# Layer-norm means one step later, chunk 0's variance at step 6, DFT pieces two a step, four group sums scaled before they are added

## The chip, the core and the metric

The kernel runs on one core of one Trainium2 chip. The metric is the device time of one execution in microseconds (us). TensorE is called PE (its weight loads PEld), VectorE DVE, ScalarE ACT, GpSimd POOL and SyncE SP.

## The reference

Three blocks follow one another, with batch 4 and 544 tokens of 512 features (32 global and 512 local ones).

```python
x = attention(q_l, k_l, v_l, q_g, k_g, v_g)        # window of 32 and global tokens, 8 heads
h = np.maximum(x @ w_in, 0.0)                      # first feed-forward block, 512 -> 1024
gate = sigmoid(conv over tokens of h)
x = (h * gate) @ w_out
mixed = np.real(fft(fft(x, axis=1), axis=2))       # second block begins here
u = x + mixed
un = (u - mean(u)) / np.sqrt(var(u) + 1e-06)
ch = np.maximum(un @ w_ch1, 0.0) @ w_ch2           # 512 -> 2048 -> 512
return u + ch
```

## The kernel before

The matmuls run on pairs of numbers, a rounded high part and the rest as a low part, so each product is three matmuls (`mm3`). PE's and SP's instructions run in the order in which the program writes them; those of DVE, ACT and POOL are ordered by a scheduler, which simulates the program with priorities per kind of work. On the chip each engine then takes its own list strictly in that order.

**The Fourier transform.** `fft(b)` (L649) is a generator of 12 pieces for each of four batches. Its matmul pieces take PSUM banks `s` and `t` in turn (`fbank`, L646), and each bank has to be read by ACT and DVE (L674 and L675, L681 and L682, or L693 and L696, L703 and L706) before the next but one piece writes it. The last piece stores `ut` into `u_d[b]`. `fstep` (L859) runs one piece. The first pieces run beside the last steps of the first feed-forward block (the loop at L871), the rest in the last phase.

**The last phase** (the loop at L898) has 80 steps `v` and two more to drain. Tokens are cut into five chunks of 436 (the last 432), and step `v` takes one block of 128 hidden features `m` of a chunk `c`, from `plan`: chunk 0 with m 0 to 7 in steps 0 to 7, chunk 1 with 0 to 7 in steps 8 to 15, chunk 0 with 8 to 15, chunk 1 with 8 to 15, then chunks 2, 3 and 4 with 16 steps each. `c_g1(v)` (g1, L804) makes 12 matmuls into bank `pv` or `g1` (the trace calls the second `ps_g`), from which ACT (L817) and DVE (L818) make the two parts `hd`. `c_g2(v - 2)` (g2, L821) makes 12 matmuls from the `hd` of two steps before into the four banks a0 to a3 (`ps_a`). After m = 7 and m = 15 a group ends: for each of the four banks DVE multiplies by the chunk's `rs` into the one buffer `tmp` (L842) and adds that to the chunk's `uc` (L843), and after m = 15 SP stores `uc`. The next group's g2 can write a bank as soon as its multiplication is done.

**The layer norm.** `ln(c)` (L758) is a generator that advances once a step: it sums a chunk over its features into `cf` and `sr` (on POOL for chunks 1 to 4, on DVE for chunk 0), has PE form the mean over partitions with two matmuls by `ones` into bank `t` (L775), subtracts it (L778), squares, sums again, and has PE form the variance in bank `s` (L792), from which ACT's square root and DVE's reciprocal (L797) make `rs`. Chunk 0's runs beside the first feed-forward block and is finished at step 0:

```python
        while v == 0 and lnq:
            step(lnq)
```

Chunks 1 to 4 begin at steps 1, 26, 36 and 52. The tiles `uc` come from a pool of three, so chunk 2 is loaded (L755) into a tile that chunk 0's output leaves free.

**The remaining weights.** m = 8 to 15 of both weight matrices (`TAIL`, 16 tiles) need the memory that the transform uses. So at one step the loop empties the queue of pieces, closes the transform's pools and has SP load the 16 tiles (L181, `raw_v`, `raw_r`, `raw_o`); in the eight steps from there `make_c` unpacks two a step (ACT L166, L169, L202; POOL L167; DVE L173, L174, L203).

Of the kernel before, what the change touches and what calls it, by code (L numbers as in the profile page):

```python
# [34 lines left out]
TAIL = [x for m in range(8, 16) for x in (m, 16 + m)]  # L35
# [92 lines left out]
def fused_kernel(ctx: ExitStack, tc: tile.TileContext, d, out):  # L128
    nc = tc.nc
    pe, act, dve, gp, sp = nc.tensor, nc.scalar, nc.vector, nc.gpsimd, nc.sync  # L130

    def pri(c):
        k = PRIORITY.get(c, 0)
        return tc.high_priority(offset=k) if k else nullcontext()

    def prio(c):
        def deco(f):
            def g(*a, **k):
                with pri(c):
                    return f(*a, **k)  # L140
            return g
        return deco

    def mm(o, a, b, start, stop):
        return pe.matmul(o, a, b, start=start, stop=stop)  # L145

    def mm3(o, ah, al, bh, bl, start, stop):
        if al is None:
            mm(o, ah, bh, start, stop)
            return  # L150
        mm(o, al, bh, start, False)
        mm(o, ah, bl, False, False)
        mm(o, ah, bh, False, stop)
# [4 lines left out]
    def f32(ap):  # L158
        return ap.bitcast(F32)
# [31 lines left out]
    def unpack(pool, t, *how):  # L191
        if mags:
            mag = mags.pop(0)
            mags.append(mag)
        else:
            mag = pool.tile([128, 512], F32, tag="mag", name="mag", bufs=2)
        from_f64(t.rearrange("p (c b) -> p c b", b=2), mag, *how)
        return mag

    def put(pool, tag, val):  # L200
        t = pool.tile([128, 2, 512], F32R, tag=tag, name="w_" + tag)
        act.copy(t[:, 0], val)  # L202
        dve.tensor_sub(t[:, 1], val, f32(t[:, 0]))  # L203
        return t
# [12 lines left out]
    def bank(tag):  # L217
        return ps.tile([128, 512], F32, tag=tag, name="ps_" + tag)
# [247 lines left out]
    g_t, acc = {}, {}  # L466
# [255 lines left out]
    def c_slot(i):  # L722
        m = i % 16
        if m < 8:
            return (wp, f"w{m + (8 if i > 15 else 0)}")
        k = TAIL.index(i) - 13
        return (vp, f"v{i}") if k < 0 else (rb, ("r0", "r1", "o")[k])

    @prio("cv")
    def fetch_c(i):  # L730
        pool, tag = c_slot(i)
        if i not in kept:
            w_raw[i] = fetch(pool, tag, c_src(i))
            return
        t = pool.tile([128, 2, 512], F32R, tag=tag, name="w_" + tag)
        sp.dma_start(f32(t), kept[i])
        (ch2 if i > 15 else ch1)[i % 16] = t

    @prio("cv")
    def make_c(i):  # L740
        t = put(*c_slot(i), unpack(mp, w_raw.pop(i), gp, True))
        (ch2 if i > 15 else ch1)[i % 16] = t

    ln_t, uc_t, rs_t, cft = {}, {}, {}, []

    def width(c):
        return min(NT, B * S - NT * c)

    def load_uc(c):
        t = uc_t[c] = up.tile([128, 5, NT], F32, tag="u", name="uc")  # L750
        a, z = NT * c, NT * c + width(c)
        while a < z:
            b, o = divmod(a, S)
            n = min(z - a, S - o)
            sp.dma_start(t[:, 0:4, a - NT * c:a - NT * c + n], u_d[b][:, :, o:o + n])  # L755
            a += n

    def ln(c):  # L758
        n = width(c)
        ut = (uc_t[c] if c else u_t[0])[:, 0:4, 0:n]  # L760
        if c == 0:
            cft.append(up.tile([128, 5, NT], F32, tag="u", name="cf"))
        cf = cft[0][:, 0:4, 0:n]
        chl = xp.tile([128, 10, NT], F32R, tag="x", name="chl")
        ch, cl, sr = chl[:, 0:4, 0:n], chl[:, 4:8, 0:n], chl[:, 8:10, 0:n]
        eng = gp if c else dve
        eng.tensor_add(cf[:, 0:2], ut[:, 0:2], ut[:, 2:4])  # L767
        eng.tensor_add(cf[:, 0], cf[:, 0], cf[:, 1])
        act.copy(sr[:, 0], cf[:, 0])
        dve.tensor_sub(sr[:, 1], cf[:, 0], f32(sr[:, 0]))  # L770
        yield
        yield
        if c == 0:
            yield
        mu = bank("t")[:, 0:n]  # L775
        mm(mu, ones, sr[:, 1], True, False)
        mm(mu, ones, sr[:, 0], False, True)
        dve.tensor_sub(cf, ut, mu[:, None, :].to_broadcast([128, 4, n]))  # L778
        act.copy(ch, cf)
        eng.tensor_sub(cl, cf, f32(ch))  # L780
        ln_t[c] = (ch, cl)
        yield
        act.activation(cf, cf, AF.Square)
        yield
        eng.tensor_add(cf[:, 0:2], cf[:, 0:2], cf[:, 2:4])
        eng.tensor_add(cf[:, 0], cf[:, 0], cf[:, 1])
        yield
        act.copy(sr[:, 0], cf[:, 0])
        dve.tensor_sub(sr[:, 1], cf[:, 0], f32(sr[:, 0]))
        yield  # L790
        yield
        va = bank("s")[:, 0:n]  # L792
        mm(va, ones, sr[:, 1], True, False)
        mm(va, ones, sr[:, 0], False, True)
        rs = rs_t[c] = uc_t[c][:, 4, 0:n] if c else rs0
        act.activation(rs, va, AF.Sqrt, bias=eps)
        dve.reciprocal(rs, rs)  # L797
        yield
# [5 lines left out]
    def c_g1(v):  # L804
        if not 0 <= v < len(plan):
            return
        c, m = plan[v]
        ch, cl = ln_t[c]
        n = width(c)
        o = bank("g1" if m % 2 else "pv")[:, 0:n]  # L810
        w = ch1[m]
        for k in range(4):
            f = slice(128 * k, 128 * k + 128)
            mm3(o, w[:, 0, f], w[:, 1, f], ch[:, k], cl[:, k], k == 0, k == 3)
        hd = lw.tile([128, 2, NT], F32R, tag="hd", name="hd", bufs=3)[:, :, 0:n]
        with pri("cev"):
            act.activation(hd[:, 0], o, AF.Relu)  # L817
            dve.scalar_tensor_tensor(hd[:, 1], o, 0.0, f32(hd[:, 0]), op0=ALU.max, op1=ALU.subtract)  # L818
        hid[v] = hd

    def c_g2(v):  # L821
        if not 0 <= v < len(plan):
            return
        c, m = plan[v]
        n = width(c)
        first, last_ = (0, 8), (7, 15)
        if c > 1:
            first, last_ = (0,), (15,)
        if m in first:
            for e in range(4):  # L830
                acc[e] = bank(f"a{e}")[:, 0:n]
        hd = hid.pop(v)
        w = ch2[m]
        for e in range(4):
            f = slice(128 * e, 128 * e + 128)
            mm3(acc[e], w[:, 0, f], w[:, 1, f], hd[:, 0], hd[:, 1], m in first, m in last_)
        if m in last_:
            uc = uc_t[c]
            tmp = cft[0][:, 4, 0:n]
            for e in range(4):  # L840
                o = uc[:, e, 0:n]
                dve.tensor_mul(tmp, acc[e], rs_t[c])  # L842
                dve.tensor_add(o, o, tmp)  # L843
                if m == 15:
                    sp.dma_start(out[128 * e:128 * e + 128, NT * c:NT * c + n], o)

    fq = [fft(b) for b in range(4)]
    lnq = []

    def step(queue, name="ln"):  # L850
        while queue:
            try:
                with pri(name):
                    next(queue[0])
                return
            except StopIteration:
                queue.pop(0)

    def fstep(n=1):  # L859
        for _ in range(n):  # L860
            step(fq, "fft")
            for c, b in ((1, 1), (0, 2)):
                if b in u_d and c not in uc_t:
                    load_uc(c)
            if 0 in u_d and not lnq and not ln_t:
                lnq.append(ln(0))
                step(lnq)
# [28 lines left out]
    rs0 = lw.tile([128, NT], F32, name="rs0")  # L896
    vp = None
    for v in range(len(plan) + 2):  # L898
        if v < 8:
            for _ in range(3):  # L900
                fstep()
            if v < 4:
                make_c(20 + v)
        if v == 8:
            while fq:
                fstep()
            right.close()
            vp = ctx.enter_context(tc.tile_pool(name="vp", bufs=1, side="right"))
            for x in TAIL:
                fetch_c(x)  # L910
        if 8 <= v < 16:
            make_c(TAIL[2 * v - 16])
            make_c(TAIL[2 * v - 15])
        while v == 0 and lnq:
            step(lnq)
        if v in (1, 26, 36, 52):
            c = {1: 1, 26: 2, 36: 3, 52: 4}[v]
            if c > 1:
                load_uc(c)
            lnq.append(ln(c))  # L920
        step(lnq)
        c_g1(v)
        c_g2(v - 2)
# [42 lines left out]
```

## Time and profile before

| | |
|---|---|
| median of the three timed runs | 840.46 us (838.49 to 842.03) |
| the profiled execution: its own time | 836.21 us |
| its span in the profile | 834.4 us |
| PE busy | 778.8 us (93%) |
| PEld busy | 710.4 us (85%) |
| DVE busy | 477.1 us (57%) |
| ACT busy | 364.5 us (44%) |
| POOL busy | 173.7 us (21%) |

A share is an average over three blocks. The last phase begins at about 402 us and the transform's first pieces lie some 60 us before that. The granted clock is given as a share of TensorE's full 2.4 GHz, so 0.50 is its lower level of 1.2 GHz, and a value between is a stretch with both.

### The profile page before, as it was taken

The numbers are of one execution on the slowest core, as the hardware profiler recorded it, in microseconds if no ns is written. First come the engines' busy times: TensorE is split into PE (matmuls) and PEld (weight loads), VectorE is DVE, ScalarE is ACT, GpSimd is POOL, SyncE is SP. The second block draws the span as 40 slices with busy tenths as digits, with TensorE's granted clock in tenths as the row PEclk, the third lists the DMA queues.
The fourth block names the chain that finished last, engine by engine and source line by source line (L and its number), as shares of the span: only waits on it lengthen the run. The fifth ranks groups of instructions, "written<-read, shape, count | busy, mean of one in ns | idle before, by whom it ended". The sixth has DMA issues, their size and how long they took to land.

```text
span 834.4 us, 13622 instructions
## 1 busy us (share of the span) xinstructions
PE 778.8 (93%) x5272; PEld 710.4 (85%) x5272; DVE 477.1 (57%) x1162; ACT 364.5 (44%) x884; POOL 173.7 (21%) x219
## 2 busy tenths in 40 slices
PE   5769999999999999989799899997999999999996
PEld 3558888888889889979689798986999999999996
DVE  5899987768776786787854877132431232213112
ACT  6677776767676775543532852112112112111110
POOL 4555442222222230000222121004013003100000
PEclk9899999999999999999899999997999999999999
DMA  7842351254126441355323900020020011001001
GB/s 252 267 150 114 127 188 38 106 191 155 31 106 204 148 129 32 105 180 191 108 97 103 353 1 1 1 76 11 22 65 0 1 49 39 1 1 43 1 1 42
DMA packets 36896, 77.80 MB, mean 93 GB/s; under 512 B 3752, under 2 KB 22056, under 8 KB 36832
## 3 DMA queue, kind: packets, MB, share of 16 engines
q1 hardware_dynamic: 36000, 74.29, 26.2%
q0 software_dynamic: 832, 2.65, 1.4%
q8 instruction: 41, 0.67, 0.4%
q14 instruction: 23, 0.19, 0.1%
HBM read 62.11 MB, written 15.20 MB: 93 GB/s over the span
## 4 chain that ended last, share of the span: by engine, by line
PE 54%; DVE 19%; DMA 14%; ACT 8%; issue 2%; SPq 2%; POOL 0%; DVEq 0%; ACTq 0%; POOLq 0%
PE ps_a L145 24%; PE ps_g L145 13%; PE ps_pv L145 11%; DMA raw_r<-in_ch_dram 9%; PE ps_s L145 4%; PE ps_t L145 3%; ACT pb L320 2%; DVE pb L308 2%; DVE y L493 2%; DMA raw_w<-in_w_in_dram 2%; DVE y L494 2%; DVE mag L174 2%; DVE mag L173 1%; DMA raw_v<-in_ch_dram 1%; ACT mag L166 1%
## 5 line engine op out<-in xcount | busy, mean ns | idle before, releaser
L145 PE MATMUL ps_g<-x,w_w 128*128 128x256 f32 (+1 forms) x768 | 113.9, 298 | 1.3 <-ACT h L482 1.0
L331 POOL TENSOR_SCALAR pb<-pb,sm 128x224 f32<-128x224 f32 x128 | 84.5, 676 | 127.9 <-DVE sm L326 81.5
L145 PE MATMUL ps_a<-g,w_w 128*128 128x254 f32 (+1 forms) x768 | 110.9, 292 | 0.0
L145 PEld LDWEIGHTS ps_g<-x,w_w 128*128 128x128 f32 x768 | 100.9, 190 | 11.0 <-issue 7.7
L145 PE MATMUL ps_a<-hd,w_w 128*128 128x436 f32 (+1 forms) x480 | 102.7, 361 | 3.4 <-DVE cf L842 3.4
L145 PEld LDWEIGHTS ps_a<-g,w_w 128*128 128x128 f32 x768 | 101.1, 190 | 0.8 <-issue 0.7
L145 PEld LDWEIGHTS ps_a<-hd,w_w 128*128 128x128 f32 x480 | 89.7, 188 | 9.9 <-DVE cf L842 5.2
L818 DVE SCALAR_TENSOR_TENSOR hd<-ps_pv,hd 128x436 fp32r<-128x436 f32 (+1 forms) x40 | 24.4, 610 | 107.3 <-ACT hd L817 107.3
L818 DVE SCALAR_TENSOR_TENSOR hd<-ps_g,hd 128x436 fp32r<-128x436 f32 (+1 forms) x40 | 24.2, 606 | 95.3 <-ACT hd L817 95.3
L145 PE MATMUL ps_a<-hd,w_v 128*128 128x436 f32 (+1 forms) x360 | 77.4, 362 | 1.4 <-DVE cf L842 1.4
L817 ACT ACTIVATE hd<-ps_g 128x436 fp32r<-128x436 f32 (+1 forms) x40 | 21.3, 533 | 119.9 <-PE ps_g L145 119.8
L145 PEld LDWEIGHTS ps_a<-hd,w_v 128*128 128x128 f32 x360 | 67.8, 189 | 6.3 <-DVE cf L842 2.5
L817 ACT ACTIVATE hd<-ps_pv 128x436 fp32r<-128x436 f32 (+1 forms) x40 | 21.3, 533 | 117.5 <-PE ps_pv L145 117.4
L320 ACT ACTIVATE pb<-pb,sm 128x224 f32<-128x224 f32 x128 | 60.4, 474 | 11.9 <-DVE sm L308 11.8
L167 POOL TENSOR_SCALAR mag<-mag 128x512 f32<-128x512 f32 x48 | 35.3, 736 | 113.3 <-ACT mag L166 112.7
L145 PE MATMUL ps_pv<-chl,w_v 128*128 128x436 f32 (+1 forms) x240 | 52.9, 370 | 0.0
L767 POOL TENSOR_TENSOR cf<-uc 128x872 f32<-128x872 f32 (+1 forms) x4 | 8.3, 2068 | 212.5 <-DMA uc<-u_d 143.0
L145 PE MATMUL ps_g<-chl,w_w 128*128 128x436 f32 (+1 forms) x240 | 52.0, 367 | 0.0
L145 PE MATMUL ps_pv<-chl,w_w 128*128 128x436 f32 (+1 forms) x240 | 50.8, 360 | 0.0
L145 PE MATMUL ps_s<-qk 64*128 64x224 f32 (+1 forms) x144 | 37.1, 411 | 13.1 <-DMA qk<-in_qk_dram 4.1
L145 PEld LDWEIGHTS ps_pv<-chl,w_v 128*128 128x128 f32 x240 | 46.8, 195 | 2.8
L145 PEld LDWEIGHTS ps_g<-chl,w_w 128*128 128x128 f32 x240 | 46.2, 193 | 2.7
(220 smaller groups left out, 1462.5 us busy)
## 6 DMA issues: line engine op xcount, KB each, us to landing
v<-in_v_dram SPq DMA_DIRECT2D x16, 640.0 KB, 4.6
qk<-in_qk_dram SPq DMA_DIRECT2D x16, 464.0 KB, 6.1
raw_r<-in_ch_dram SPq DMA_DIRECT2D x14, 512.0 KB, 6.5
raw_v<-in_ch_dram SPq DMA_DIRECT2D x13, 512.0 KB, 9.3
kept<-w_o SPq DMA_DIRECT2D x12, 512.0 KB, 5.5
w_w<-kept SPq DMA_DIRECT2D x12, 512.0 KB, 3.2
qk<-in_qk_dram SPq DMA_DIRECT2D x16, 304.0 KB, 6.1
u_d<-u SPq DMA_DIRECT2D x4, 1088.0 KB, 5.3
```

The source lines that it names most:

```text
L145: return pe.matmul(o, a, b, start=start, stop=stop)
L166: act.activation(mag, f32(head), AF.Abs, scale=65536.0)
L167: (clamp or dve).tensor_scalar(mag, mag, TOP, 2.0, op0=ALU.min, op1=ALU.max)
L173: dve.scalar_tensor_tensor(val, val, 3, tail, op0=ALU.logical_shift_left, op1=ALU.bitwise_or)
L174: dve.scalar_tensor_tensor(val, head, -(2**31), val, op0=ALU.bitwise_and, op1=ALU.bitwise_or)
L308: anchor[i] = dve.tensor_tensor_reduce(out=pbs(i)[h][:, a, 0:224], in0=sb[h][:, a], in1=mask[:, 2 * where(i)[1] + a], scale=-0.125, scalar ...
L320: act.activation(p, p, AF.Exp, bias=sm[:, k:k + 1], scale=-1.0, accum_out=sm[:, 4 + k:5 + k])
L331: gp.tensor_scalar(p, p, sm[:, k:k + 1], 1.0, op0=ALU.mult, op1=ALU.mult)
L493: dve.scalar_tensor_tensor(y, hb[:, cc - 1:cc - 1 + n], convw2[:, m, 0:1], y, op0=ALU.mult, op1=ALU.add)
L494: dve.scalar_tensor_tensor(y, hb[:, cc + 1:cc + 1 + n], convw2[:, m, 2:3], y, op0=ALU.mult, op1=ALU.add)
L817: act.activation(hd[:, 0], o, AF.Relu)
L818: dve.scalar_tensor_tensor(hd[:, 1], o, 0.0, f32(hd[:, 0]), op0=ALU.max, op1=ALU.subtract)
```

## The change

1. All chunks now wait three steps between the sum and the mean, where chunks 1 to 4 waited two. Chunk 0's mean goes to bank `pv` and not `t`.
2. At a group end `tmp` becomes four buffers (the rows 0 to 3 of `cf`), and the program writes four multiplications and then four additions.
3. The transform's pieces come two a step in steps 0 to 8, where they came three a step in steps 0 to 7. The first four `make_c` stand at steps 2 to 5 and not 0 to 3, and the closing of the pools, the 16 loads and the unpacking all come one step later.
4. What is left of chunk 0's layer norm (its variance) runs at step 6 and not at step 0.

```diff
--- before.py
+++ after.py
@@ -770,9 +770,8 @@
         dve.tensor_sub(sr[:, 1], cf[:, 0], f32(sr[:, 0]))
         yield
         yield
-        if c == 0:
-            yield
-        mu = bank("t")[:, 0:n]
+        yield
+        mu = bank("t" if c else "pv")[:, 0:n]
         mm(mu, ones, sr[:, 1], True, False)
         mm(mu, ones, sr[:, 0], False, True)
         dve.tensor_sub(cf, ut, mu[:, None, :].to_broadcast([128, 4, n]))
@@ -836,11 +835,12 @@
             mm3(acc[e], w[:, 0, f], w[:, 1, f], hd[:, 0], hd[:, 1], m in first, m in last_)
         if m in last_:
             uc = uc_t[c]
-            tmp = cft[0][:, 4, 0:n]
+            tmp = cft[0][:, 0:4, 0:n]
+            for e in range(4):
+                dve.tensor_mul(tmp[:, e], acc[e], rs_t[c])
             for e in range(4):
                 o = uc[:, e, 0:n]
-                dve.tensor_mul(tmp, acc[e], rs_t[c])
-                dve.tensor_add(o, o, tmp)
+                dve.tensor_add(o, o, tmp[:, e])
                 if m == 15:
                     sp.dma_start(out[128 * e:128 * e + 128, NT * c:NT * c + n], o)
 
@@ -896,23 +896,25 @@
     rs0 = lw.tile([128, NT], F32, name="rs0")
     vp = None
     for v in range(len(plan) + 2):
-        if v < 8:
-            for _ in range(3):
-                fstep()
-            if v < 4:
-                make_c(20 + v)
-        if v == 8:
+        if v < 9:
+            fstep(2)
+            if 2 <= v < 6:
+                make_c(18 + v)
+        if v == 9:
             while fq:
                 fstep()
             right.close()
             vp = ctx.enter_context(tc.tile_pool(name="vp", bufs=1, side="right"))
             for x in TAIL:
                 fetch_c(x)
-        if 8 <= v < 16:
-            make_c(TAIL[2 * v - 16])
-            make_c(TAIL[2 * v - 15])
-        while v == 0 and lnq:
-            step(lnq)
+        if 9 <= v < 17:
+            make_c(TAIL[2 * v - 18])
+            make_c(TAIL[2 * v - 17])
+        if v == 0:
+            ln0, lnq = lnq, []
+        if v == 6:
+            while ln0:
+                step(ln0)
         if v in (1, 26, 36, 52):
             c = {1: 1, 26: 2, 36: 3, 52: 4}[v]
             if c > 1:
```

Three places show how this moves the engines' instructions. The first is PE's order at step 0. `c1` and `s1` are the transform's second tables, `ab` its intermediate, `ones` the mean's or variance's matrix, `chl` the normalized chunk and `w_w0`, `w_w1` its weights. Before:

```order
L145 MATMUL ps_s_5127<-c1_4344,ab_5026 128x274 x9
L145 MATMUL ps_t_5139<-s1_4345,ab_5026 128x274 x9
L145 MATMUL ps_s_5161<-chl_4664,ones_62 128x436 x2
L145 MATMUL ps_pv_5166<-chl_4664,w_w0_4471 128x436 x12
L145 MATMUL ps_s_5182<-c1_4344,ab_5026 128x274 x9
L145 MATMUL ps_t_5194<-s1_4345,ab_5026 128x274 x9
L145 MATMUL ps_s_5208<-c1_4344,ab_5026 1x274 x9
L145 MATMUL ps_g1_5237<-chl_4664,w_w1_4541 128x436 x12
```

and with the change:

```order
L145 MATMUL ps_s_5127<-c1_4344,ab_5026 128x274 x9
L145 MATMUL ps_pv_5139<-chl_4664,w_w0_4471 128x436 x12
L145 MATMUL ps_t_5155<-s1_4345,ab_5026 128x274 x9
L145 MATMUL ps_s_5169<-c1_4344,ab_5026 128x274 x9
L145 MATMUL ps_g1_5186<-chl_4664,w_w1_4541 128x436 x12
L145 MATMUL ps_t_5202<-s1_4345,ab_5026 128x274 x9
L145 MATMUL ps_s_5216<-c1_4344,ab_5026 1x274 x9
L145 MATMUL ps_pv_5240<-chl_4664,w_w2_4610 128x436 x12
```

The variance has left this place, and a g1 stands after the first, the third and the fifth of these pieces, where one stood after the second and one after the fifth.

The second is DVE's order at the end of chunk 0's second group (step 25). Before:

```order
L842 TENSOR_TENSOR cf_4663<-ps_a0_6076,rs0_5116 128x436
L818 SCALAR_TENSOR_TENSOR hd_6273<-ps_g1_6260,hd_6273 128x436
L843 TENSOR_TENSOR uc_5222<-uc_5222,cf_4663 128x436
L842 TENSOR_TENSOR cf_4663<-ps_a1_6077,rs0_5116 128x436
L843 TENSOR_TENSOR uc_5222<-uc_5222,cf_4663 128x436
L842 TENSOR_TENSOR cf_4663<-ps_a2_6078,rs0_5116 128x436
L843 TENSOR_TENSOR uc_5222<-uc_5222,cf_4663 128x436
L818 SCALAR_TENSOR_TENSOR hd_6321<-ps_pv_6308,hd_6321 128x436
L842 TENSOR_TENSOR cf_4663<-ps_a3_6079,rs0_5116 128x436
L843 TENSOR_TENSOR uc_5222<-uc_5222,cf_4663 128x436
```

and with the change:

```order
L840 TENSOR_TENSOR cf_4663<-ps_a0_6076,rs0_5116 128x436
L817 SCALAR_TENSOR_TENSOR hd_6273<-ps_g1_6260,hd_6273 128x436
L840 TENSOR_TENSOR cf_4663<-ps_a1_6077,rs0_5116 128x436
L843 TENSOR_TENSOR uc_5230<-uc_5230,cf_4663 128x436
L840 TENSOR_TENSOR cf_4663<-ps_a2_6078,rs0_5116 128x436
L840 TENSOR_TENSOR cf_4663<-ps_a3_6079,rs0_5116 128x436
L843 TENSOR_TENSOR uc_5230<-uc_5230,cf_4663 128x436 x3
L817 SCALAR_TENSOR_TENSOR hd_6321<-ps_pv_6308,hd_6321 128x436
```

Before, an addition follows each multiplication, and the last pair stands behind the next step's `hd_6321`; now all eight operations stand ahead of it, with one addition before the last two multiplications.

The third is PE's order at chunk 2's mean (`ones`). Before:

```order
L145 MATMUL ps_a_6327<-hd,w_v_5689 128x436 x3
L145 MATMUL ps_t<-chl,ones 128x436 x2
L145 MATMUL ps_pv<-chl,w_v_5825 128x436 x12
L145 MATMUL ps_a_6324<-hd,w_v_5741 128x436 x3
L145 MATMUL ps_a_6325<-hd,w_v_5741 128x436 x3
L145 MATMUL ps_a_6326<-hd,w_v_5741 128x436 x3
L145 MATMUL ps_a_6327<-hd,w_v_5741 128x436 x3
L145 MATMUL ps_g_6403<-chl,w_v_5869 128x436 x12
```

and with the change:

```order
L145 MATMUL ps_a_6327<-hd,w_v_5725 128x436 x3
L145 MATMUL ps_pv<-chl,w_v_5853 128x436 x12
L145 MATMUL ps_a_6324<-hd,w_v_5773 128x436 x3
L145 MATMUL ps_a_6325<-hd,w_v_5773 128x436 x3
L145 MATMUL ps_a_6326<-hd,w_v_5773 128x436 x3
L145 MATMUL ps_a_6327<-hd,w_v_5773 128x436 x3
L145 MATMUL ps_t<-chl,ones 128x436 x2
L145 MATMUL ps_g_6402<-chl,w_v_5897 128x436 x12
```

One whole step, a g1 and a g2, has moved ahead of the mean's two matmuls.

## Rows read from the trace of the kernel before

**Rows 1.** The page: the span.

```profile
span 834.4 us, 13622 instructions
```

**Rows 2.** Waits of PE from 340 us on: total us, times, longest.

```profile
PE ps_t L145 <- DVE chl L770: 7.7, 2, 6.7
PE ps_s L145 <- DVE u L696: 4.8, 1, 4.8
PE ps_a L145 <- DVE cf L842: 4.8, 5, 1.4
PE ps_t L145 <- DVE cf L778: 2.1, 1, 2.1
PE ps_t L145 <- DVE ab L675: 0.9, 1, 0.9
```

**Rows 3.** Chain of waits, one step: start us, us, what.

```profile
479.13 2.38 PE ps_g L145 x12
481.52 2.38 PE ps_a L145 x12
```

**Rows 4.** PE's timeline and windows (PE PEld DVE ACT POOL, clock) at chunk 0's mean.

```profile
365.83 0.66 PE L145 MATMUL ps_t<-chl,ones 128*128 128x436 f32 x2 [0.97 <-DVE chl L770]
368.56 0.36 PE L145 MATMUL ps_t<-c,fl 128*92 128x258 f32 x1 [2.06 <-DVE cf L778]
...
370.00:372.00 2.00, 2.00 (x11) 2.00 (x12) 1.78 (x1) 0.45 (x2) 0.00 (x0) 0.60 0.01 2
372.00:374.00 2.00, 2.00 (x11) 2.00 (x11) 0.61 (x3) 1.77 (x2) 0.00 (x0) 0.54 0.22 39
```

**Rows 5.** Windows of the stage with the DFT in steps 0 to 9.

```profile
414.00:416.00 2.00, 2.00 (x10) 1.35 (x8) 2.00 (x5) 0.12 (x1) 0.00 (x0) 0.50 0.00 0
416.00:418.00 2.00, 2.00 (x7) 1.82 (x6) 2.00 (x5) 1.10 (x2) 1.35 (x1) 0.50 0.00 0
...
401.00:471.00 70.00, 64.16 (x353) 58.34 (x352) 46.19 (x75) 30.45 (x53) 17.90 (x13) 0.95 0.40 139
```

**Rows 6.** Timelines of DVE (379 and 404 to 408 us) and of POOL (first, fourth).

```profile
379.59 0.72 DVE L658 TENSOR_TENSOR ff<-u 128x548 f32<-128x548 f32 x1
...
404.07 1.53 DVE L658 TENSOR_TENSOR ff<-u 128x548 f32<-128x548 f32 x1
408.17 2.86 DVE L797 RECIPROCAL rs<-rs 128x436 f32<-128x436 f32 x1
...
400.77 2.09 POOL L767 TENSOR_TENSOR cf<-uc 128x872 f32<-128x872 f32 x1 [69.48 <-DVE ff L655]
404.99 1.09 POOL L167 TENSOR_SCALAR mag<-mag 128x512 f32<-128x512 f32 x1
```

**Rows 7.** PE's last DFT piece; the chain's store; ACT's first raw weight.

```profile
445.65 0.55 PE L145 MATMUL ps_t<-c,ab 92*1 92x274 f32 x3
...
448.83 4.60 DMA u_d<-u
...
458.05 0.66 ACT L166 ACTIVATE mag<-raw_v 128x512 f32<-128x512 f32 x1 [3.38 <-DMA raw_v<-in_ch_dram]
```

**Rows 8.** DVE's timeline at chunk 0's last group end; windows after chunk 2's mean.

```profile
555.56 0.61 DVE L818 SCALAR_TENSOR_TENSOR hd<-ps_pv,hd 128x436 fp32r<-128x436 f32 x1 [0.38 <-ACT hd L817]
556.09 0.60 DVE L842 TENSOR_TENSOR cf<-ps_a,rs 128x436 f32<-128x436 f32 x1
556.73 0.61 DVE L843 TENSOR_TENSOR uc<-uc,cf 128x436 f32<-128x436 f32 x1
...
570.00:572.00 2.00, 2.00 (x7) 1.84 (x6) 1.76 (x1) 0.00 (x0) 0.00 (x0) 0.50 0.03 8
572.00:574.00 2.00, 2.00 (x8) 1.81 (x6) 0.21 (x1) 1.65 (x1) 0.00 (x0) 0.50 0.00 0
```

**Rows 9.** Chain of waits at the program's end, first and last of eight.

```profile
825.86 0.62 DVE cf L842
...
830.56 0.61 DVE uc L843
```

## The prediction

> **What bounds the kernel now.** I read the page first: a span of 834.4 us [rows 1], inside a profiled execution of 836.2 us; the three timed runs have a median of 840.5 us, 4.3 us more, so the sum below is made against 836.2 and then moved to the median. TensorE (PE) is busy nearly everywhere after 100 us, so what can be won late in the program is the time in which it stands still, and the time in which it is granted the lower clock. Second I read the list of PE's waits from 340 us to the end [rows 2]: five lines, 20.3 us in all, each of them ended by VectorE (DVE). Third, the chain of waits through an undisturbed step of the last phase [rows 3]: 12 matmuls of g1 in 2.38 us and 12 of g2 in 2.38 us, 4.76 us a step. The chain is PE with these holes in it. The reader should see that the holes belong to four places, which the four parts of the change touch one by one. Last I read PE's timeline and short windows around each hole for the granted clock.
>
> **Chunk 0's mean moves from bank t to bank pv.** Today PE computes it in bank t and the next DFT piece in t waits 2.06 us for the subtraction that reads the mean; a wait of 0.97 us stood just before [rows 4]. Behind both, the windows 370 to 372 and 372 to 374 have PE busy throughout at a granted clock of 0.60 and 0.54, largely the lower of its levels, 1.2 instead of 2.4 GHz: 2 x 0.40 + 2 x 0.46 = 1.7 us of work lost [rows 4]. In pv nothing of the DFT waits for that subtraction. The first wait (for the sum that feeds the mean) stays. Gain 2.1 + 1.7 = 3.8 at most, nothing at least; I take 3.0, near the upper end, because PE's waits list shows no other hole there, and keep 0.8 back because DVE has the same work in less time.
>
> **Chunk 0's variance to step 6 and DFT pieces two a step.** At steps 0 to 5 three pieces stand together, and PE's order begins with pieces s, t, the variance in s, one g1, then three pieces in a row. PE stops for 4.8 us until L696 has emptied bank s, and then works through 414 to 418 without a break at a granted clock of 0.50: 4 x 0.5 = 2.0 us lost [rows 2, 5]. Ahead of L696 in DVE's queue stood the reciprocal of chunk 0's variance, 2.86 us [rows 6], which nobody needs before chunk 0's first group end. Now it goes to step 6, and a g1 of 2.38 us stands between pieces that share a bank two further on. DVE's work is moved, not less: 46.2 us in the 70 us from 401 to 471 [rows 5], so it fits. The wait for L675 (0.9 us) [rows 2] remains: chunk 1's mean still follows a piece in its own bank t. Gain 4.8 + 2.0 = 6.8; against it I set 1.0, one more wait of the L675 kind, as PE's order now has pieces that DVE empties only just in time: 5.8. Bounds: 1.0, if the stall only moves, to 6.8.
>
> In this stage DVE and POOL (GpSimd) also get in each other's way. L658, an addition of two SBUF tensors, took 1.53 us beside POOL's operations and 0.72 us at another time [rows 6], so 0.81 more; of those POOL operations there are four from 400.8 to 406.1 [rows 6]. The change leaves them there. The Trainium skill's page "SBUF — State Buffer", section "SBUF: two separate sides", says that this port is a lock, held by whichever began first for its whole instruction. By that page each POOL operation could hold a DVE operation of that kind for its whole length; the trace agrees that they slow each other, and it shows less than a whole length. What four such meetings would do is the second rival.
>
> **Four scaled group sums, then the additions.** Each of seven group ends has four multiplications (which free the four banks) and four additions, today alternating through one buffer. PE waits for a bank there five times, 4.8 us in all [rows 2]; now the multiplications come earlier in DVE's order. I take all 4.8, as g1's 2.38 us covers what four multiplications of 0.6 us take; bounds 0 and 4.8. At the very end, eight alternating operations start from 825.86 to 830.56, 0.67 us apart [rows 9], since each pair depends on the one before; two independent ones start 0.53 apart (555.56 and 556.09) and dependent ones 0.64 (556.09 and 556.73) [rows 8]. Seven distances of 0.53 in place of 0.67 are 1.0 us; four stores stand closer together, so I take 0.8, between -0.4 and 1.0.
>
> **Means of chunks 1 to 4 one step later.** Only chunk 2 has a hole: its chunk is loaded into the tile that chunk 0's output frees, and PE stands still 6.7 us in front of the mean's two matmuls [rows 2]; 570 to 574 then run at 0.50, 2.0 us lost [rows 8]. One step later, PE has 4.76 us of matmuls to do in that hole. The last addition also moves: today it starts at 556.73, behind hd at 555.56 [rows 8]; in the new order all four additions come before that hd, so store, load and mean are 1.2 us earlier. Left: 6.7 - 4.76 - 1.2 = 0.7 us, shorter than the 0.97 and 2.06 us after which the clock fell only when both stood together. Gain 6.7 - 0.7 + 2.0 = 8.0; bounds 4.0 (the step alone, less a slower store) and 8.7. Its first g1 comes at step 32, three steps behind the new mean, so nothing is late there. The other chunks show no wait for a mean to win or lose.
>
> **What is late next.** The last DFT piece moves from step 5 to step 8. Behind it hang the last store of the transform (DVE's finish at 448.83 against PE's last piece at 445.65, then 4.60 us), then SP's 16 loads of the remaining weights; ACT waited for the first of these until 458.05 [rows 7], 12.4 us behind the start of that piece. In ACT's order two of these loads now stand ahead of step 10's Relu, whose bank PE needs again at step 12, four steps (19 us) behind that piece: 12.4 us and four ACT operations of 0.66 us [rows 7] fit. Price if they don't: up to a step, 4.8 us. I take -1.0, near the upper bound of nothing.
>
> **Sum:** 3.0 + 5.8 + 4.8 + 0.8 + 8.0 - 1.0 = 21.4 us. 836.2 - 21.4 = 814.8; on the median 840.5 - 21.4 = 819.1, so 819.
>
> **The rivals.** (1) Half of it: DVE stays the bound from 365 to 425 us, and the waits come back at other pieces. For it: DVE is busy 2.00 of 2.00 us in both windows at 414 and 416 [rows 5]. Against: 46.2 of 70 us overall. Without the first two terms 12.6 us are left: 828. (2) The lock: four POOL operations at 0.81 us each hold DVE 3.2 us, 2.2 more than the 1.0 allowed, on PE's path: 821 to 822. (3) The reorder does less than it says: DVE's order at chunk 0's end has an addition before the last two multiplications. Half of the 4.8 us and the 1.2 us of the store go: 819 + 3.6 = 823. (4) Slower: 17 DFT pieces with matmuls run in steps 0 to 8, each now alone between g1 and g2; if DVE, strictly in its order, empties each bank late, PE waits 17 times. At 2.06 us, the longest wait of a DFT piece for its bank's reader outside the big hole [rows 4], that is 35 us, so 854; it decides from 21.4 / 17 = 1.26 us a piece. For it: the L675 wait of 0.9 us. Against: between two pieces of one bank lie a g1 and mostly a g2, 4.76 us, for two or three DVE operations.
>
> **Chances.** The forecast (814 to 823, with rivals 2 and 3 at its edge: 0.58 for the sum itself, 0.06 for the lock, 0.06 for the reorder) 0.70; half of it, 824 to 832, 0.20; nothing measurable, all holes filled by new ones, 0.05; slower 0.05. A measurement of this kernel tells about 0.5% (4.2 us) from no change, so faster 0.90, same 0.05, slower 0.05. Range: all best ends together give 3.8 + 6.8 + 4.8 + 1.0 + 8.7 = 25.1 us, 815.4, and half the spread of the runs (1.8 us) brings 813.5; upwards it takes in rival 1 with its 828 and ends at 829.
>
> **What would show it.** Right: PE's waits from 340 us on fall from 20.3 us to under 6; no wait for the mean's subtraction and none for L696; the wait before chunk 2's mean under 1.5 us, and no window there at half clock; the steps 0 to 8 end about 6 to 7 us earlier relative to their start. Wrong: a list of PE waits on DVE at the DFT's banks adding up to more than 5 us; ACT's Relu behind the raw weights delaying g1 at steps 12 to 16; a granted clock of 0.5 after a short wait.

## The result and the profile after

The changed kernel takes 813.82 us (median of three runs, 812.65 to 814.58) against 839.48 us for the kernel before on the same chip: ratio 0.9691, 95% interval 0.9653 to 0.973. A fourth run, of 1893.61 us, is left out. The forecast was 819 us in a range of 813.5 to 829, so the time lies at the range's lower end. Four more runs (e0) gave 813.08 us, just below it, and 0.9661 [0.9638, 0.9684]. The profiled execution took 812.65 us.

The page of the changed kernel, its span and first busy shares [rows 1]:

```profile
span 810.8 us, 13615 instructions
PE 770.1 (95%) x5272; PEld 705.6 (87%) x5272; DVE 476.6 (59%) x1162; ACT 363.3 (45%) x884; POOL 175.6 (22%) x219
```

DVE is busy as long as before (476.6 and 477.1 us), PE 770.1 us where it was 778.8. What went is idle time of PE, and the half clock that stretched its work. PE's waits from 340 us on in the changed kernel (total, times, longest) answer to [rows 2]:

```profile
PE ps_t L145 <- DVE chl L770: 2.1, 1, 2.1
PE ps_pv L145 <- DVE chl L770: 1.0, 1, 1.0
PE ps_t L145 <- DVE ab L675: 0.9, 1, 0.9
PE ps_t L145 <- DVE u L706: 0.4, 1, 0.4
```

4.4 us are left of 20.3. The waits for the mean's subtraction, for L696 and for a group end's multiplication are all gone. PE's timeline shows where the four stand, and two windows (PE PEld DVE ACT POOL, clock) lie behind chunk 0's mean [rows 4]:

```profile
368.54 0.66 PE L145 MATMUL ps_pv<-chl,ones 128*128 128x436 f32 x2 [0.97 <-DVE chl L770]
...
408.15 1.38 PE L145 MATMUL ps_t<-s,ab 92*128 92x274 f32 x9 [0.43 <-DVE u L706]
...
424.31 0.66 PE L145 MATMUL ps_t<-chl,ones 128*128 128x436 f32 x2 [0.92 <-DVE ab L675]
...
555.44 0.66 PE L145 MATMUL ps_t<-chl,ones 128*128 128x436 f32 x2 [2.07 <-DVE chl L770]
```

```profile
370.00:372.00 2.00, 2.00 (x15) 1.83 (x15) 1.91 (x3) 1.13 (x2) 0.00 (x0) 1.00 1.02 420
372.00:374.00 2.00, 2.00 (x18) 2.00 (x17) 1.07 (x1) 1.89 (x4) 0.00 (x0) 1.00 0.67 178
```

These windows ran at 0.60 and 0.54 before and run at full clock now, 15 and 18 matmuls in each where there were 11. In windows of 20 and 40 us from 340 to 800 us the changed kernel's granted clock is 1.00 throughout.

To place the gain I took the same six instructions in both profiles; a row's first number is its start. PE's timeline of the kernel before:

```profile
360.28 0.35 PE L145 MATMUL ps_t<-co,fl 1*92 1x258 f32 x1
...
400.56 1.32 PE L145 MATMUL ps_s<-c,ab 92*128 92x274 f32 x9
...
471.00 2.53 PE L145 MATMUL ps_pv<-chl,w_w 128*128 128x436 f32 x12
...
478.97 2.54 PE L145 MATMUL ps_g<-chl,w_w 128*128 128x436 f32 x12
...
552.40 2.56 PE L145 MATMUL ps_pv<-chl,w_v 128*128 128x436 f32 x12
...
577.13 2.55 PE L145 MATMUL ps_g<-chl,w_v 128*128 128x436 f32 x12
```

and of the changed kernel:

```profile
362.99 0.35 PE L145 MATMUL ps_t<-co,fl 1*92 1x258 f32 x1
...
399.34 1.32 PE L145 MATMUL ps_s<-c,ab 92*128 92x274 f32 x9
...
462.67 2.53 PE L145 MATMUL ps_pv<-chl,w_w 128*128 128x436 f32 x12
...
467.43 2.55 PE L145 MATMUL ps_g<-chl,w_w 128*128 128x436 f32 x12
...
538.91 2.55 PE L145 MATMUL ps_pv<-chl,w_v 128*128 128x436 f32 x12
...
555.94 2.55 PE L145 MATMUL ps_g<-chl,w_v 128*128 128x436 f32 x12
```

| stretch between these | before | after | gained | its term in the prediction |
|---|---|---|---|---|
| start of the program | 360.28 | 362.99 | -2.7 | none |
| chunk 0's mean | 40.28 | 36.35 | 3.9 | 3.0 |
| the DFT in steps 0 to 8, raw weights | 70.44 | 63.33 | 7.1 | 5.8 - 1.0 |
| chunk 0's first group end | 7.97 | 4.76 | 3.2 | of 4.8 |
| up to chunk 0's second group end | 73.43 | 71.48 | 2.0 | of 4.8 |
| chunk 2's mean | 24.73 | 17.03 | 7.7 | 8.0 |
| other group ends, program's end | 257.27 | 254.86 | 2.4 | rest of 4.8, and 0.8 |

The sum is 23.6 us, the difference of the spans. The first line is not the change's: nothing before that place was touched, and in eleven profiles of kernels alike up to there the matmuls of chunk 0's mean begin anywhere from 365.50 to 370.50 us. From that place on the change gained 26.3 us.

### The profile page after: what moved, and what is told of

It is laid out like the page before. It is cut to its first block, busy times and chain, and to the rows that moved or that the text cites. A ratio compares the mean times of both kernels' runs of the same rounds, so it can differ in the third digit from the quotient of the medians.

```text
span 810.8 us, 13615 instructions
## 1 busy us (share of the span) xinstructions
PE 770.1 (95%) x5272; PEld 705.6 (87%) x5272; DVE 476.6 (59%) x1162; ACT 363.3 (45%) x884; POOL 175.6 (22%) x219
## 4 chain that ended last, share of the span: by engine, by line
PE 57%; DVE 19%; DMA 11%; ACT 9%; issue 2%; SPq 1%; POOL 1%; DVEq 0%; ACTq 0%; POOLq 0%
PE ps_a L145 25%; PE ps_g L145 14%; PE ps_pv L145 11%; DMA raw_r<-in_ch_dram 8%; PE ps_s L145 3%; PE ps_t L145 3%; ACT pb L320 3%; DVE y L493 2%; DMA raw_w<-in_w_in_dram 2%; DVE pb L308 2%; DVE y L494 2%; DVE mag L174 2%; DVE mag L173 1%; DVE y L511 1%; ACT y L500 1%
## 5 line engine op out<-in xcount | busy, mean ns | idle before, releaser
L167 POOL TENSOR_SCALAR mag<-mag 128x512 f32<-128x512 f32 x48 | 38.3, 798 | 193.4 <-ACT mag L166 192.9
L817 DVE SCALAR_TENSOR_TENSOR hd<-ps_g,hd 128x436 fp32r<-128x436 f32 (+1 forms) x40 | 24.3, 608 | 92.9 <-ACT hd L816 92.9
L817 DVE SCALAR_TENSOR_TENSOR hd<-ps_pv,hd 128x436 fp32r<-128x436 f32 (+1 forms) x40 | 24.2, 606 | 91.7 <-ACT hd L816 91.7
L145 PE MATMUL ps_pv<-chl,w_v 128*128 128x436 f32 (+1 forms) x240 | 50.8, 360 | 0.0
L145 PEld LDWEIGHTS ps_pv<-chl,w_v 128*128 128x128 f32 x240 | 45.1, 188 | 2.5
L145 PEld LDWEIGHTS ps_pv<-chl,w_w 128*128 128x128 f32 x240 | 44.9, 188 | 2.5
```

Source lines behind the costliest of these rows:

```text
L167: (clamp or dve).tensor_scalar(mag, mag, TOP, 2.0, op0=ALU.min, op1=ALU.max)
```

## The experiments

Ratios are to the kernel before on the same chip, with 95% intervals. Diffs of e1 to e7 and of e9 are against the changed kernel (that of e9 shows only what differs from e6), those of e8 and e10 against the kernel before. Times of e1 to e4 are compared with the changed kernel's first ratio, 0.9691, those of e5, e6 and e9 with e0's 0.9661; by the other of the two each would come out 2.5 us different. A profile's own differences are counted from chunk 0's mean on, since that begins at another time in each.

### e1: chunk 0's mean back in bank t

```diff
-        mu = bank("t" if c else "pv")[:, 0:n]
+        mu = bank("t")[:, 0:n]
```

> Only chunk 0's mean goes back to bank t. Theory (the bank is what held PE): the 2.06 us wait of the next DFT piece for the mean's subtraction returns, behind the 0.97 us wait that is still there, and with it some 3 us at about half the granted clock, so 3.5 to 4 us slower than the changed kernel: about 818. Rival (the place was won by the other parts, or DVE's work is the bound there): the wait moves elsewhere and the time stays within 1 us of 814.

817.42 us, 0.9727 [0.967, 0.9783]: 0.36% or 3.0 us slower than the changed kernel by the ratios, whose intervals overlap; the trace has to carry it. PE's timeline, and a window behind it:

```profile
371.47 0.52 PE L145 MATMUL ps_t<-c,fl 128*92 128x258 f32 x1 [2.06 <-DVE cf L777]
```

```profile
372.00:374.00 2.00, 2.00 (x8) 1.43 (x8) 0.87 (x1) 1.33 (x2) 0.00 (x0) 0.50 0.26 96
```

The wait of 2.06 us and the half clock come back together, with no other part of the change undone. The bank is the cause of this term. Its size by the trace is more than 3.0 us: the stretch from 363.19 to 404.56 us takes 41.4 us, where the changed kernel's takes 36.35. The profiled run is 6.0 us longer in all, 1.7 of them at chunk 2's mean, where half clock followed a wait of 2.17 us and the changed kernel's 2.07 us had none behind it.

### e2: three pieces a step, and e3: the variance back at step 0

```diff
-        if v < 9:
-            fstep(2)
-            if 2 <= v < 6:
-                make_c(18 + v)
-        if v == 9:
+        if v < 8:
+            for _ in range(3):
+                fstep()
+            if v < 4:
+                make_c(20 + v)
+        if v == 8:
```

(in e2, with the unpacking one step earlier too), and

```diff
-        if v == 6:
+        if v == 0:
             while ln0:
```

in e3.

> Pieces three a step again in steps 0 to 7, loads and unpacking one step earlier, with the variance still at step 6. Theory (the reciprocal ahead of the drains was the larger half of the 4.8 us wait): one new wait of 1 to 2 us for L696 near 410 us, no stretch at half clock, and part of the bank waits at step 9's group end as the raw weights come earlier; 1.5 to 4 us slower, 816 to 818. Rival (the density of the pieces was the cause): the wait of 4 us or more and the half clock are back, 6 us or more slower, over 820.

> Only chunk 0's variance goes back to step 0, pieces stay two a step. Theory (the reciprocal, 2.9 us in DVE's queue ahead of the drains, which had no room to spare: one wait of 0.4 us already): PE waits 2.5 to 4.5 us for a DFT bank between 405 and 412 us, perhaps with 1 to 2 us at half clock; 3 to 6 us slower, 817 to 820. Rival (density of the pieces): under 1 us slower.

e2 took 815.53 us, 0.9708 [0.9664, 0.9752], 1.4 us slower than the changed kernel by the ratios; e3 819.16 us, 0.9747 [0.9703, 0.9791], 4.7 us slower. The intervals of both overlap the changed kernel's 0.9653 to 0.973; that of e3 lies apart from e0's. PE's timeline of e2 and of e3, with the starts of two instructions from the tables above:

```profile
397.57 1.32 PE L145 MATMUL ps_s<-c,ab 92*128 92x274 f32 x9
...
407.74 2.21 PE L145 MATMUL ps_s<-c,ab 92*1 92x274 f32 x9 [2.83 <-DVE u L696]
...
465.26 2.52 PE L145 MATMUL ps_pv<-chl,w_w 128*128 128x436 f32 x12
```

```profile
400.16 1.32 PE L145 MATMUL ps_s<-c,ab 92*128 92x274 f32 x9
...
411.94 2.29 PE L145 MATMUL ps_t<-s,ab 92*128 92x274 f32 x9 [1.80 <-DVE u L706]
...
469.22 2.53 PE L145 MATMUL ps_pv<-chl,w_w 128*128 128x436 f32 x12
```

Both bring a hole back, and a stretch at half clock behind it, which for e2 I had not expected (0.50 from 408 to 412 us; in e3 0.50 to 0.51 from 412 to 418). In this stage e2 takes 67.7 and e3 69.1 us, against 63.3 in the changed kernel and 70.4 before: undoing the pieces alone costs 4.4 us there, undoing the variance alone 5.7, and the two together won 7.1. So neither part does it alone, and their shares do not add. In e3 the reciprocal of 2.86 us [rows 6] stands in front of the pieces' readers in DVE's queue again, and a piece waits 1.80 us; a wait of 0.97 us before it is that of the variance's own matmuls, for bank `s`. In e2 the wait for L675 is gone, but with its raw weights one step earlier it loses another 1.4 us at chunk 0's first group end. Both profiles get 1.3 us back at chunk 2's mean, where PE waits only 0.8 us: chunk 2's load landed in 4.47 and 4.48 us and not in 5.76, which the edits do not explain.

### e4: multiplications and additions alternating again

```diff
-            tmp = cft[0][:, 0:4, 0:n]
-            for e in range(4):
-                dve.tensor_mul(tmp[:, e], acc[e], rs_t[c])
+            tmp = cft[0][:, 4, 0:n]
             for e in range(4):
                 o = uc[:, e, 0:n]
-                dve.tensor_add(o, o, tmp[:, e])
+                dve.tensor_mul(tmp, acc[e], rs_t[c])
+                dve.tensor_add(o, o, tmp)
```

> Only the group ends go back to one buffer and alternating multiplications and additions. Theory: the bank waits come back at the ends of steps 9, 17 and 33 (4.8 us in all before; perhaps only 2 to 4 us as the raw weights now come later than step 9's end), the last output tail is 1 us longer, and chunk 2's load starts 1.2 us later: its mean waits 3 us and not 2.07; together 4 to 7 us slower, 818 to 821. Rival (the waits at the group ends came from the raw weights' unpacking in the same queues, which now comes later anyway): step 9's end has no wait, and only the tail and chunk 2 are left, 2 us slower.

825.89 us, 0.9835 [0.9788, 0.9882]: 1.44% or 12 us slower than the changed kernel, twice what I expected. PE's waits, and two windows:

```profile
PE ps_a L145 <- DVE cf L841: 6.4, 5, 2.2
```

```profile
470.00:472.00 2.00, 2.00 (x7) 1.81 (x7) 1.11 (x2) 1.91 (x4) 0.61 (x1) 0.52 1.03 377
...
564.00:566.00 2.00, 2.00 (x7) 1.82 (x6) 1.58 (x1) 0.38 (x1) 0.00 (x0) 0.52 0.00 0
```

The waits for a bank are 6.4 us, more than the 4.8 of the kernel before. The one of 2.18 us at chunk 0's first group end is followed by half clock, which the kernel before's profile did not show there: 1.7 us lost in 465 to 475 (0.83 over 10 us). Chunk 2's mean waits 2.75 us (0.7 more) and loses another 1.7 us in 560 to 570; the end is 0.9 us longer. 6.4 + 1.7 + 0.7 + 1.7 + 0.9 = 11.4 us, of 13.5 by which this profile is longer than the changed kernel's.

### e5: the means of chunks 1 to 4 one step earlier again

```diff
         yield
         yield
-        yield
+        if c == 0:
+            yield
         mu = bank("t" if c else "pv")[:, 0:n]
```

It ran beside the changed kernel itself (e0, the 813.08 us above), whose profile shows the same four waits again, of 2.28, 0.97, 0.92 and 0.66 us.

> The changed kernel once more, for comparison with the three below on the same chip. Any theory: 0.969 of the kernel before, 0.965 to 0.973; its five waits... no other wait of PE than the four of its first profile (2.07, 0.97, 0.92 and 0.43 us, 4.4 in all).

> Means of chunks 1 to 4 one step earlier again, the rest of the change kept. Theory (PE gets 4.76 us of matmuls to do in the hole before chunk 2's mean): that wait becomes 2.07 + 4.76 = 6.8 us, and a stretch at half clock follows that costs 2 to 3 us; chunk 1's mean waits no longer than 2 us. 5 to 8 us slower than the changed kernel, 0.976 to 0.979 of the kernel before. Rival (the load ends last whatever PE does meanwhile, and work only moves behind it): wait of 6.8 us but no change of the time, 0.969.

819.12 us, 0.9731 [0.9704, 0.9758], 0.70% or 5.9 us slower than e0's 0.9661. PE's timeline and a window:

```profile
416.11 0.66 PE L145 MATMUL ps_t<-chl,ones 128*128 128x436 f32 x2 [2.45 <-DVE ab L675]
...
552.79 1.09 PE L145 MATMUL ps_t<-chl,ones 128*128 128x436 f32 x2 [5.54 <-DVE chl L770]
```

```profile
554.00:556.00 2.00, 2.00 (x7) 1.81 (x7) 1.89 (x1) 0.07 (x1) 0.00 (x0) 0.50 0.00 0
```

The theory holds: the wait and the half clock at chunk 2's mean are back. The wait is 5.54 and not 6.8 us because chunk 2's load landed in 4.51 us here and in 5.98 us in e0. That chunk 1's mean would wait no longer than 2 us was wrong; it waits 2.45 us.

### e8 and e10: one part alone

e8 is the kernel before with its means of chunks 1 to 4 one step later, e10 the kernel before with the sums scaled ahead of the additions (the same lines as in e4, the other way round). The diff of e8:

```diff
         yield
         yield
-        if c == 0:
-            yield
+        yield
         mu = bank("t")[:, 0:n]
```

> The kernel before with nothing but the means of chunks 1 to 4 one step later. Theory (the parts add up): chunk 2's wait falls by 4.76 us from 6.7 to about 2.0 us, or 3.5 if its load takes 6.0 us as in some of the runs above; no half clock behind it. 4.8 to 6.8 us faster, 0.992 to 0.994 of the kernel before. Rival (the wait is only pushed on): the same 6.7 us in all at two places, no change.

> The kernel before with nothing but the four scaled sums ahead of the four additions. Theory (the waits listed are all that it wins): the 4.8 us of waits behind L842 go, chunk 2's store is 1.2 us earlier, the end 0.8 to 1.0 us shorter: 6.8 to 7.0 us faster, 0.992 of the kernel before. Rival (the order is worth what its undoing cost in the changed kernel): 12 us faster, 0.986.

e8 took 840.42 us, 0.9992 [0.9975, 1.0009]: nothing at all. e10 took 829.76 us, 0.9864 [0.9835, 0.9893], 11.4 us faster. PE's timeline of e8:

```profile
479.26 0.82 PE L145 MATMUL ps_a<-hd,w_w 128*128 128x436 f32 x3 [1.09 <-ACT raw_v L169]
483.06 2.75 PE L145 MATMUL ps_a<-hd,w_w 128*128 128x436 f32 x6 [2.97 <-DVE cf L841]
486.60 1.46 PE L145 MATMUL ps_a<-hd,w_w 128*128 128x436 f32 x3 [0.79 <-DVE cf L841]
...
580.99 1.10 PE L145 MATMUL ps_t<-chl,ones 128*128 128x436 f32 x2 [3.16 <-DVE chl L770]
```

and DVE's, in the same place:

```profile
474.57 2.88 DVE L796 RECIPROCAL uc<-uc 128x436 f32<-128x436 f32 x1 [0.99 <-ACT uc L795]
...
478.51 0.61 DVE L841 TENSOR_TENSOR cf<-ps_a,rs 128x436 f32<-128x436 f32 x1
...
482.39 0.61 DVE L841 TENSOR_TENSOR cf<-ps_a,rs 128x436 f32<-128x436 f32 x1
```

At chunk 2's mean e8 wins what it should: 6.75 us of wait become 3.16 (its load took 5.58 us), and that stretch is 5.0 us shorter, though half clock (0.51 from 582 to 584 us) still follows the wait, which I had not expected. But chunk 1's variance has moved one step too, and its reciprocal of 2.88 us now ends at 477.45, right in front of chunk 0's first group end, where DVE also unpacks the raw weights. With multiplications and additions alternating, the second multiplication comes 3.9 us behind the first. PE waits 4.85 us there in all, 1.09 of them for a raw weight, where it waited 2.70 us before, and runs at a clock of 0.50 from 482 to 490; that stretch takes 12.2 us where it took 7.97. The later means pay only if the group end can take the crowding, and the new order of the sums is what makes it do so: in the changed kernel there is no wait at that place. There the raw weights also come a step later, but that is not the reason: in e2, which has the later means and the new order and unpacks the raw weights as early as e8, no multiplication keeps PE waiting there, only a raw weight for 0.76 us.

e10 is worth 11 us alone and 12 us when it is undone last (e4), where I had put 4.8 + 0.8 us and 1.2 us of an earlier store. Its own profile against that of the kernel before shows 7.9 us from chunk 0's mean on: 834.4 - 829.3 = 5.1, and it began 2.8 us later (368.65 against 365.83). Another 1.2 us shows at chunk 0's mean, which e10 leaves alone: behind the same waits of 0.97 and 2.06 us the profiles of e1, e8 and e10 lose more to half clock, and take 41.3 to 41.5 us over the stretch that took 40.28 in the kernel before. The rest, too, lies in the kernel before, whose profiled execution took less than any of its 35 other runs (836.21 against 837.48 to 843.67 us), with a mean granted clock of 0.980, where the 15 runs beside e10 had 0.967 to 0.979. That those runs fell to half clock behind the waits at the group ends, as e4 and e8 do, fits; no profile of such a run was taken, so this is argued for the group ends and not shown.

### e6: three means later still, and e7, a try at POOL

```diff
-        yield
-        yield
-        yield
-        mu = bank("t" if c else "pv")[:, 0:n]
+        for _ in range(4 if c in (0, 2) else 3):
+            yield
+        mu = bank(("pv", "s")[c] if c < 2 else "t")[:, 0:n]
```

e7 begins chunk 1's layer norm at step 3 and not at step 1.

> Chunk 0's and chunk 2's means yet another step later, and chunk 1's mean in bank s instead of t. Theory (each of the three waits is PE reaching an instruction too early): the waits of 2.07, 0.97 and 0.92 us go, 4.0 us in all, and the time falls by 3 to 5 us against the changed kernel, to 0.964 or 0.965 of the kernel before. Rival: chunk 2's normalized chunk, which POOL finishes 8.2 us after the mean, comes too late for g1 at step 32, and PE waits there instead: no change or 1 to 3 us slower, 0.970 to 0.973; or chunk 1's mean in s holds up a transform piece in s by up to 2 us.

> The kernel with three later means once more, for comparison with the next on the same chip: 0.9626 of the kernel before, 0.960 to 0.965, with a wait of 1.2 us behind L706 and no other after 340 us.

> Chunk 1's layer norm, whose sums POOL forms, begins at step 3 instead of 1. Theory (DVE's additions of the transform are slowed by the POOL operation beside them): DVE's L657 of 1.85, L658 of 1.65 and L173 of 1.09 us at 401 to 406 us fall to 0.7 to 0.8 us where no POOL operation lies beside them, about 2.4 us of DVE in all; others two steps later that then meet POOL's sums become longer, and the wait of 0.43 us behind L706 goes. Time within 1.5 us of the changed kernel, since PE waited only 0.4 us there. Rival (these operations are long because of their operands or of what stands before them): they keep their 1.6 to 1.9 us without POOL beside them.

e6 took 810.06 us, 0.9626 [0.9603, 0.9649], and in five more runs on another chip 809.19 us, 0.9626 [0.9602, 0.9651]; 2.9 us faster than the changed kernel (e0) by the ratios to before, whose intervals overlap slightly. The three waits are gone, and that behind L706 has grown from 0.4 to 1.0 and 1.2 us. Neither rival came true.

e7 (813.09 us, a single run) told nothing of its question. SP and POOL wait for no step: they took chunk 1's load and sums as soon as the data were there. L767 began 0.2 us behind the first g1 (402.31 against 402.10), in the changed kernel 0.1 us (400.57 against 400.50), and L657 and L658 took 1.99 and 1.65 us beside POOL as before. Moving a step in the program moves only what PE's order holds back.

### e9: e6, with chunk 1's two sums on DVE

```diff
         eng = gp if c else dve
-        eng.tensor_add(cf[:, 0:2], ut[:, 0:2], ut[:, 2:4])
-        eng.tensor_add(cf[:, 0], cf[:, 0], cf[:, 1])
+        esum = gp if c > 1 else dve
+        esum.tensor_add(cf[:, 0:2], ut[:, 0:2], ut[:, 2:4])
+        esum.tensor_add(cf[:, 0], cf[:, 0], cf[:, 1])
```

> The kernel with three later means, and chunk 1's first two sums on DVE in place of POOL. Theory (POOL's sums slow DVE's operations on SBUF beside them): L657 of 1.9 to 2.1 us and L658 of 1.65 us fall to 0.72 us, L173 keeps up to 1.09 us where POOL's L167 lies beside it; 2.5 us less on DVE against some 1.8 us for the two sums, so DVE reaches L706 up to 0.7 us earlier, its wait of 1.2 us falls to 0.5 to 1.2 us, and the time is within 1 us of the kernel with three later means. Rival (they are long without POOL too): L657 and L658 keep their times, L706 comes 1.8 us later, PE waits 3 us there and half clock follows: 2 to 4 us slower.

807.73 us, 0.9604 [0.9583, 0.9625]. DVE's timeline of e6 (its second run), POOL's beside it, and DVE's of e9:

```profile
398.74 2.48 DVE L657 TENSOR_TENSOR fl<-ff,fh 128x548 fp32r<-128x548 f32 x1
401.14 1.09 DVE L173 SCALAR_TENSOR_TENSOR mag<-mag,raw_w 128x512 int32<-128x512 int32 x1
402.16 1.64 DVE L658 TENSOR_TENSOR ff<-u 128x548 f32<-128x548 f32 x1
```

```profile
398.54 2.09 POOL L767 TENSOR_TENSOR cf<-uc 128x872 f32<-128x872 f32 x1 [0.97 <-DMA uc<-u_d]
400.61 1.08 POOL L167 TENSOR_SCALAR mag<-mag 128x512 f32<-128x512 f32 x1
401.66 1.55 POOL L768 TENSOR_TENSOR cf<-cf 128x436 f32<-128x436 f32 x1
```

```profile
399.49 0.72 DVE L657 TENSOR_TENSOR fl<-ff,fh 128x548 fp32r<-128x548 f32 x1
400.12 1.06 DVE L768 TENSOR_TENSOR cf<-uc 128x872 f32<-128x872 f32 x1
401.10 0.69 DVE L173 SCALAR_TENSOR_TENSOR mag<-mag,raw_w 128x512 int32<-128x512 int32 x1
401.70 1.14 DVE L658 TENSOR_TENSOR ff<-u 128x548 f32<-128x548 f32 x1
402.77 0.60 DVE L769 TENSOR_TENSOR cf<-cf 128x436 f32<-128x436 f32 x1
```

With the sums on POOL three DVE operations take 2.48 + 1.09 + 1.64 = 5.21 us. With the sums on DVE the same three take 0.72 + 0.69 + 1.14 = 2.55, and the two sums 1.06 + 0.60 = 1.66: DVE does more work in 1.0 us less. PE's list of waits from 340 us on is empty; I had expected 0.5 to 1.2 us to be left behind L706. e9 is the fastest version, below the changed kernel (0.9661 [0.9638, 0.9684] for e0) beyond the intervals; against e6 they overlap, so that last step of some 2 us is not settled by the times.

## Why the prediction was right, and where its sums were off

**The reading held.** Four places, each with PE idle on DVE and half clock behind three of them, and each part of the change met its place. The forecast of waits under 6 us, of none on L696 or on the subtraction, of full clock behind chunk 2's mean, and of steps 0 to 8 some 6 to 7 us shorter all came out: 4.4 us, none, 1.00, 7.1 us. Only the wait before chunk 2's mean, called under 1.5 us, is 2.07. The sum was 21.4 us; the medians give 839.48 - 813.82 = 25.7, the profiles 26.3 from 360 us on. The sum was 4 us short: the time lies just below the forecast's 814 to 823 and just inside the range. Point by point:

**Chunk 0's mean, 3.0 predicted, 3.9 found.** The upper end of 3.8. The 0.8 us held back for DVE's crowding was not lost. The half clock was priced from the kernel before's profile, 1.7 us; in e1 the wait of 2.06 us and the half clock behind it cost 5.0 us in this stretch.

**Variance and pieces, 5.8 predicted, 7.1 found.** This includes the raw weights' term. Of the allowance of 1.0 only a wait of 0.43 us behind L706 appeared. The 1.0 us for the later raw weights was not lost: ACT took the first one at 463.36 us, 11.8 us behind the start of the last piece at 451.60 (12.4 before), and no PE wait followed.

**Group ends and program's end, 4.8 + 0.8 predicted, 7.6 found** (3.2 + 2.0 + 2.4; the program's end is 0.9 of it), and 11 to 12 us by the times of e10 and e4. This was the term most undersized. I priced it by the waits in one execution, the shortest of its 36 on record. I did not ask what other waits at those places would do to the clock, nor what a crowded group end would do to the other parts.

**Means later, 8.0 predicted, 7.7 found.** The size is right for reasons that partly cancel. The half clock gave 3.0 and not 2.0 us (7.7 less the 6.75 - 2.07 of the wait). The wait left is 2.07 and not 0.7 us. The store was indeed earlier: the last addition ended 4.9 us behind the mark at 552.40 before and 3.2 us behind that at 538.91 after. But store and load took longer. The chain of waits before:

```profile
557.37 1.93 DMA out_dram<-uc
560.04 4.43 DMA uc<-u_d
```

and after:

```profile
542.12 2.12 DMA out_dram<-uc
544.98 5.76 DMA uc<-u_d
```

The step that failed is "the step alone, less a slower store": I took a slower transfer into the bounds and not into the value. And e8 shows that the later means alone leave the time as it was. The prediction added four terms as if each stood alone; they do not, and the sum came out because the sums' order was among them.

**The rivals.** (1), the waits coming back at other pieces, did not happen; nor did (3), the reorder doing less, or (4), a wait at each of 17 pieces: the waits left in that stage are 0.43 and 0.92 us. The pieces do not stand alone between g1 and g2, as (4) has it, but mostly in pairs between a g2 and the next g1. (2), the lock, is real on DVE and small on PE: L657, L173 and L658 took 1.85, 1.09 and 1.65 us in the changed kernel where 0.72, 0.68 and 0.72 are their own times, 2.47 us more in all, and PE waited 0.43 us behind them.

## What to carry to other kernels

A stall of two microseconds on a busy TensorE can be worth its own length or nearly three times that, because of the half clock that may follow: 2.07 us in the changed kernel had none behind it, 1.80 us in e3 had 3.4 us of lost work. The mean granted clock of one kernel differed from run to run (0.961 to 0.980); price a stall by both, and compare the profiled run's mean clock with that of the timed runs before trusting its sum. Parts that share an engine's queue do not add: moving work one step later filled one hole here and opened another at a crowded group end, until the order inside that group end was changed too. A short elementwise job given to POOL is no relief for DVE where both read SBUF at the same time; count what it adds to DVE's operations beside it.

## What the runs showed of the hardware that I had not expected

**DVE's additions of two SBUF tensors wait for the end of POOL's operation, to the last tenth.** The prediction said that the trace shows less than a whole length. It shows the whole rest: L657 or L658, begun while a POOL operation ran, took the time to that operation's end, plus its own length, less 0.13 us. So it was in all 27 such meetings from 395 us on in the 14 profiles, within 0.03 us. In e6, L657 began at 398.74 and POOL's L767 ended at 400.63: 1.89 + 0.72 - 0.13 = 2.48, as measured. L658 and L768 there: 1.05 + 0.72 - 0.13 = 1.64. In e9, L658 beside POOL's L167 (401.23 + 1.03): 0.56 + 0.72 - 0.13 = 1.15 against 1.14. In the kernel before, L658's 1.53 us [rows 6] follows the same way from L768's end at 405.01. The Trainium skill's page "SBUF — State Buffer", section "SBUF: two separate sides", calls the shared port a lock held for a whole instruction by whichever began first; the trace agrees. It goes the other way too: POOL's L167, 0.61 us by itself, took 3.41 us at 409.40 in the changed kernel, beside a row of DVE operations that kept their own lengths (L173 at 409.87 took 0.67 us). And DVE operations that read a PSUM bank were not held: L817 took its usual 0.61 us at 560.26, inside POOL's L779 of 3.95 us.

**The length of one wait does not say whether the clock falls.** The clock fell to 0.50 behind waits of 1.80 us (e3), 2.17 us (e1), 2.18 us (e4), 2.75 us (e4) and 2.83 us (e2), and stayed at 1.00 behind 2.07 us in the changed kernel, 2.28 us in e0 and 2.45 us in e5. Three of these, 2.07, 2.17 and 2.28 us, are the same wait at chunk 2's mean. What else decides was not tried.

**The same load took 4.4 to 6.0 us.** Chunk 2's load of 440 KB, with only the chunk's other part of 432 KB beside it, landed in 4.43 us in the kernel before, 4.45, 4.47, 4.48, 4.51 and 4.64 us in e10, e2, e3, e5 and e7, but 5.16 in e4, 5.58 in e8 and 5.76, 5.98 and 5.87 us in the changed kernel, e0 and e1. Of these eleven profiles an instruction fetch falls into that load in all but those of the kernel before, e5 and e10. These three are among the short loads, but so are e2, e3 and e7. The cause is open.
